# Conv plus ELU feed-forward on one core: the taps' load moves to GpSimd's queue, and the warming matmuls read another tile

## The chip, the cores and the metric

The kernel runs on one core of a Trainium2 chip. A core has TensorE (PE; matmuls and their weight loads), VectorE (DVE), ScalarE (ACT), GpSimd (POOL) and SyncE (SP, which only issues transfers). Each engine works through its own queue of instructions in order, and the queues meet at semaphores. Transfers are issued from the queues of SyncE, ScalarE and GpSimd and are carried by 16 DMA engines. The metric is the device time of one execution in microseconds, median of several runs; lower is better.

## The reference

`x` is (8, 4096, 192), `weight` (8, 7). First a depthwise causal convolution along the sequence: the 192 columns are 8 heads of 24, each head has 7 taps, which are the softmax of its row of `weight`. Then a feed-forward step over all 32768 tokens: 192 to 2048, ELU, 2048 to 192.

```python
w = np.exp(weight - np.max(weight, axis=-1, keepdims=True))
w = w / (np.sum(w, axis=-1, keepdims=True) + 1e-09)              # (8, 7)
x_pad = np.concatenate([np.zeros((B, 6, D)), x], axis=1)
out = np.einsum('hk,bskhg->bshg', w, windows of x_pad)           # 7 taps back
h = out.reshape(B * S, D) @ w_in
g = np.where(h > 0.0, h, np.exp(np.minimum(h, 0.0)) - 1.0)
return (g @ w_out).astype(np.float32)
```

## The kernel before

It is written instruction by instruction for each engine, with semaphores by hand: one function for each of the five queues. The order of TensorE's work in the steady part is a list, `steps`, made ahead of time; nothing at run time changes it.

The tokens are cut into 32 tiles of 1024. Each tile passes 16 blocks of 128 columns of the hidden layer; a step n is one block of one tile, in two halves of 512 tokens (u = 0, 1). For each half, TensorE makes `H` by three matmuls (`w_in` against `att`, line 754), ScalarE takes its exponential into `E` (line 543), GpSimd cuts it at 1 (line 471), VectorE takes the larger of `E - 1` and `H` into `gT` (line 610), and TensorE multiplies `gT` by `w_out` (line 788) into `ops`, which ScalarE copies out. `H` has six banks of PSUM, so TensorE may be ahead of VectorE by six halves and no more.

The convolved tokens `att` of tiles 1 to 31 come from matmuls of `x` (`xg`) with a band matrix `Tm` of the taps (line 732), copied by ScalarE (line 521) and turned by a transposing transfer. Those of tile 1 stand in TensorE's queue at steps 7 to 10, those of tile 2 from step 13.

The first tile goes another way, so that it starts early. This is the part that matters here; the line numbers are of the kernel before:

- The first 1024 rows of x come in two loads of 512 rows into `xf` (`load_first`, line 340): ScalarE's queue issues the first half as its first instruction, SyncE's queue the second half, behind the load of the taps (`wh`, line 802; 8 rows of 28 bytes).
- VectorE begins with memsets: `zw` (zeros, 128 x 512, line 553), `sel`, `ident`, and three more. GpSimd makes an identity matrix of `ident` and a selection matrix of `sel` (lines 431 and 440), then waits for the taps (line 449), and then issues its loads in this order: `w_in` in three column groups of two loads each (line 425), both pieces of x of tile 1 (`xg`, line 398), `w_out` (line 455), both pieces of x of tile 2. Only then comes its loop of cutting at 1.
- The softmax of the taps: VectorE takes the row maximum (line 562, waits for the taps) and subtracts it (564), ScalarE takes the exponential (488), VectorE makes the reciprocal (568) and the tap tile `zt` (570). In ScalarE's queue the exponential stands ahead of the cast of its half of x (490); in VectorE's queue these four stand ahead of the cast of its half (578).
- SyncE writes `zw` and then `zt` into a DRAM tensor (lines 805, 810) and reads it back as the band matrix `Tm` (815).
- TensorE: 18 warming matmuls (line 639) whose results nobody reads; one small matmul that spreads the taps over the partitions (646, waits for `zt` and for GpSimd's two selects); 12 small matmuls for the halos (652, wait for ScalarE's cast); 24 transposes of x (665, wait for VectorE's cast); two more warming matmuls; 48 conv matmuls in three groups of 16 (686), which wait for VectorE's diagonal matrices `Dg` (580) and for copies of the transposed x (499 on ScalarE, 587 on VectorE); then the list `steps`. In its first seven blocks the list also has 12 warming matmuls (line 704), which read `zw`.

The warming matmuls of line 639 read a constant tile of ones, which the program makes before the block begins:

```python
WARM = (18, 1, 2)
one = nc.const_aps.tensor(1.0, [P, HP * QUAD], BF16)     # 128 x 256
```

`W(sem, value)` makes the engine wait until a semaphore has reached a value; a wait that is already known to be met is left out.

Of the kernel before, what the change touches and what calls it, by code (L numbers as in the profile page):

```python
# [8 lines left out]
BF16 = mybir.dt.bfloat16  # L9
# [3 lines left out]
P = 128  # L13
HP = 64
# [22 lines left out]
RUN = 2  # L37
WCOLS = ((0, 256), (256, 1024), (1024, 2048))
Q_PART = (0,) * 2 + (1,) * 6 + (2,) * 8
WARM = (18, 1, 2)  # L40

CONV_AT = ((0, 1, 1, 0), (4, 1, 1, 1), (9, 2, 0, 0), (12, 2, 0, 1))
EARLY_CONV = ((7, 1, 0, 0), (8, 1, 0, 1), (9, 1, 1, 0), (10, 1, 1, 1), (13, 2, 0, 0), (14, 2, 0, 1))
# [4 lines left out]
QUAD = 4  # L48
# [6 lines left out]
def bass_lightweight_conv__then__act_elu_kernel(  # L55
# [167 lines left out]
    with ExitStack() as stack:  # L223
# [32 lines left out]
        zw = sbuf("zw", [P, GS], BF16)  # L256
# [136 lines left out]
        @block.gpsimd  # L393
        def _gpsimd(g: bass.BassGpSimd):
            W = Waits(g)

            def load_x(s, part):
                g.dma_start(  # L398
                    xg[:, s % NXB, WPG * part : WPG * (part + 1), :],
                    bass.AP(  # L400
                        tensor=x_flat.tensor,
                        offset=(s * SUP + GS * part - PAD) * D,
                        ap=[[D, P], [TOK * D, WPG], [1, D]],
                    ),
                ).then_inc(s_x[s % NXB][part], 16)

            def pad_x(s):
                x_ready(W, s, 0)
                g.memset(xg[0:PAD, s % NXB, 0, :], 0.0).then_inc(s_z)

            def copy_x(s):
                W(s_cv, 4 * (s - NXB - 1) + 1)
                if s == NXB + 1:
                    g.dma_start(  # L414
                        xb[s * SUP - 8 : s * SUP, :], x_flat[s * SUP - 8 : s * SUP, :]
                    ).then_inc(s_xb[s % 2], 16)
                g.dma_start(  # L417
                    xb[s * SUP : (s + 1) * SUP, :].rearrange("(p t) d -> p (t d)", p=P),
                    x_flat[s * SUP : (s + 1) * SUP, :].rearrange("(p t) d -> p (t d)", p=P),
                ).then_inc(s_xb[s % 2], 16)  # L420

            def load_w_in(k, halves):
                c0, c1 = WCOLS[k]
                for r in halves:
                    g.dma_start(  # L425
                        w_in[HP * r : HP * (r + 1), :, c0:c1],
                        moe_w_in.rearrange("(p j) f -> p j f", j=3)[:, :, c0:c1],
                    ).then_inc(s_w[k], 16)

            W(s_one, 1)  # L430
            g.affine_select(
                out=ident[:],
                in_=ident[:],
                pattern=[[-1, P]],
                compare_op=ALU.is_equal,
                fill=0.0,
                base=0,
                channel_multiplier=1,
            ).then_inc(s_id)
            g.affine_select(  # L440
                out=sel[:].rearrange("p (r h c) -> p r h c", r=2, h=HEADS),
                in_=sel[:].rearrange("p (r h c) -> p r h c", r=2, h=HEADS),
                pattern=[[0, 2], [-1, HEADS], [0, 8]],
                compare_op=ALU.is_equal,
                fill=0.0,
                base=0,
                channel_multiplier=1,
            ).then_inc(s_id)
            W(s_wd, 16)
            load_w_in(0, (0, 1))  # L450
            load_w_in(1, (0, 1))
            load_w_in(2, (0, 1))
            load_x(1, 0)
            load_x(1, 1)
            g.dma_start(
                w_out.rearrange("p (q r) d -> p q (r d)", r=RUN),
                moe_w_out.rearrange("(q p r) d -> p q (r d)", p=FC, r=RUN),
            ).then_inc(s_w[3], 16)
            load_x(2, 0)
            load_x(2, 1)  # L460
            for n in range(NP):
                s, i = divmod(n, NQ)
                if i == X_PAD and s + 2 < NS and (s + 2) % SPB == 0:
                    pad_x(s + 2)
                if i == X_COPY and s and s + 3 < NS:
                    copy_x(s + 3)
                if n == X_LATE[0]:
                    copy_x(3)
                for u in range(2):
                    W(s_exp, 2 * n + u + 1)  # L470
                    g.tensor_scalar(  # L471
                        out=E[:, n % NE, u, :],
                        in0=E[:, n % NE, u, :],
                        scalar1=1.0,
                        scalar2=0.0,
                        op0=ALU.min,
                        op1=ALU.max,
                    ).then_inc(s_clp)
# [141 lines left out]
        def _tensor(pe):  # L620
# [11 lines left out]
                else:  # L632
                    W(s_ce, 2 * was[1] + was[2] + 1)

            one = nc.const_aps.tensor(1.0, [P, HP * QUAD], BF16)

            def warm(count):
                for _ in range(count):
                    pe.matmul(  # L639
                        ops[:, 0, 0 : HP * QUAD], one[:, 0:P], one, start=True, stop=True  # L640
                    )

            warm(WARM[0])
            W(s_id, 2)
# [17 lines left out]
            for j in range(3):  # L662
# [8 lines left out]
                            tile_position=(0, HP * r),  # L671
                        )
                ins.then_inc(s_tp)
            warm(WARM[2])
            W(s_D, 1)
            W(s_z0, 2)
            for j in range(3):
# [18 lines left out]
                            tile_position=(HP * r, 0),  # L696
                        )
                ins.then_inc(s_hc)
            W(s_zw, 1)
            seen = {}  # L700
            for x_, op in enumerate(steps):
                if op[0] == "w":
# [96 lines left out]
        @block.sync  # L799
        def _sync(sy):  # L800
            W = Waits(sy)
            sy.dma_start(wh[:], weight[:, :]).then_inc(s_wd, 16)
            load_first(sy, 1)
            W(s_zw, 1)
            sy.dma_start(
                bass.AP(tensor=taps.tensor, offset=0, ap=[[(HEADS + 2) * CW, BANDS], [(HEADS + 1) * CW, 2], [1, CW]]),
                zw[0:BANDS, 0 : 2 * CW].rearrange("p (a e) -> p a e", a=2),
            ).then_inc(s_band, 16)
            W(s_wp, 1)
            sy.dma_start(  # L810
                bass.AP(tensor=taps.tensor, offset=CW, ap=[[CW, HEADS], [(HEADS + 2) * CW, BANDS], [1, CW]]),
                zt[:, :].unsqueeze(1).to_broadcast([HEADS, BANDS, CW]),
            ).then_inc(s_band, 16)
            W(s_band, 32)
            sy.dma_start(
                Tm[:, :, :].rearrange("p h e -> p (h e)"),
                bass.AP(tensor=taps.tensor, offset=CW + TAP + KSIZE - 1, ap=[[(HEADS + 2) * CW - P // BANDS, BANDS], [-1, P // BANDS], [1, HEADS * CW]]),
            ).then_inc(s_band, 16)

            def load_cast(s):  # L820
                W(s_cv, 4 * (s - NXB))
                W(s_xb[s % 2], 16 * ((s - 1) // 2 + (s % 2)))
                if s > NXB + 1:
                    W(s_xb[(s - 1) % 2], 16 * ((s - 2) // 2 + ((s - 1) % 2)))
                for part in range(2):
                    row = s * SUP + GS * part - PAD
                    for w0, w1, rows in ((0, WPG - 1, P), (WPG - 1, WPG, GS - TOK * (WPG - 1) + PAD)):
                        v0 = WPG * part
                        sy.dma_start(
                            xg[0:rows, s % NXB, v0 + w0 : v0 + w1, :],  # L830
                            bass.AP(
                                tensor=xb.tensor,
                                offset=(row + TOK * w0) * D,
                                ap=[[D, rows], [TOK * D, w1 - w0], [1, D]],
                            ),
                        ).then_inc(s_xq[s % NXB][part], 16)

            for x_, op in enumerate(steps):
                if op[0] == "h" and op[2:] == (0, 0):
                    s, i = divmod(op[1], NQ)  # L840
                    if i == X_LOAD and s and s + 3 < NS:
                        load_cast(s + 3)
                    if op[1] == X_LATE[1]:
                        load_cast(3)
                elif op[0] == "c" and op[3:] == (1, HB - 1):
                    m, b = op[1:3]
                    s = m // 2 + 1
                    if m % 2 and b:
                        conv_read(W, m)
                        for u in range(2):  # L850
                            W(s_h[u], NQ * (s - 1))
                        turn_att(sy, s)
                elif x_ in stops:
                    acc = acc_of(op)
                    t, half, kb, g = acc
                    if (t, half) == (last, 1):
                        if (kb, g) != (1, 1):
                            taken(W, acc)
                            out_group(sy, t, half, g, kb)
                    else:  # L860
                        taken(W, acc)
                        out_group(sy, t, half, g)
            for b in range(2):
                sy.wait_ge(s_out[b], 32 * NS + 32 * b)
# [28 lines left out]
```

## Time and profile before

| what | value |
|---|---|
| median of 3 runs | 724.81 us (724.77 to 725.16) |
| profiled execution, its own time | 724.81 us |
| its span (first to last instruction) | 722.7 us |
| TensorE matmul busy | 716.8 us, 99% of the span |
| VectorE busy | 651.2 us, 90% |
| ScalarE busy | 655.9 us, 91% |
| GpSimd busy | 631.3 us, 87% |
| first H matmul (line 754) begins | 11.29 us |
| first E (ScalarE), first gT (VectorE) | 12.48 us, 13.82 us |
| x of the first tile used: ScalarE's half, SyncE's half | 3.88 us, 5.15 us |

Times inside the profile are counted from the first instruction of the execution. A row of the timeline gives start, length, engine, line, operation, what it writes and reads, how many instructions are merged, and in brackets how long the engine was idle before and what ended that. [...] A busy TensorE is not a TensorE at its peak. "issue" as a reason for idle time means that no engine is seen to end it; a landing transfer may be what ended it. The time from issue to landing of a transfer is in the part on DMA, as a median over the transfers in a row.

### The profile page before, as it was taken

To read this page: it belongs to the slowest core of one execution; us is meant where nothing else is said; L and a number is where in the kernel's file an instruction comes from. 1 tells how busy PE (TensorE), PEld (TensorE's weight loads), DVE (VectorE), ACT (ScalarE), POOL (GpSimd) and SP (SyncE) were. 2 spreads that over 40 slices of the span, in tenths; PEclk is the share of its full clock that TensorE was granted. 3 is DMA by queue.
4 is the path that set the end of the run, shared out by engine and by line. 5 is a ranking of instruction groups with operands and counts; after the bars stand their busy time and mean duration, and the time that the engine had idled before them with its cause. 6 is when DMAs were issued, how large, how long until landed. Compare 5 with 4: busy or idle time off the path is not lost.

```text
span 722.7 us, 28745 instructions
## 1 busy us (share of the span) xinstructions
PE 716.8 (99%) x11877; PEld 622.0 (86%) x11877; DVE 651.2 (90%) x1043; ACT 655.9 (91%) x1286; POOL 631.3 (87%) x1078
## 2 busy tenths in 40 slices
PE   9999999999999999999999999999999999999998
PEld 5598888888888888888888888888888888888897
DVE  4889999999999999999999999999999999999995
ACT  5999999999999999999999999999999999999994
POOL 7889888889888889888889888898888898888893
PEclk9999999999999999999999999999999999999999
DMA  9855533555544634344545345444346454542212
GB/s 175 128 119 84 117 71 95 117 93 93 99 87 95 116 80 106 90 97 95 113 74 110 77 95 116 100 87 111 75 95 117 87 100 97 91 94 71 57 36 68
DMA packets 130051, 69.16 MB, mean 96 GB/s; under 512 B 94128, under 2 KB 128688, under 8 KB 129456
## 3 DMA queue, kind: packets, MB, share of 16 engines
q1 hardware_dynamic: 123760, 52.08, 31.3%
q0 software_dynamic: 5872, 14.75, 15.1%
q8 instruction: 93, 1.52, 0.8%
q10 hardware_dynamic: 288, 0.49, 0.2%
q14 instruction: 38, 0.31, 0.1%
HBM read 43.51 MB, written 36.61 MB: 111 GB/s over the span
## 4 chain that ended last, share of the span: by engine, by line
PE 96%; DVE 1%; ACT 1%; POOL 1%; DMA 1%; issue 0%; SPq 0%; ACTq 0%
PE ops L788 51%; PE H L754 40%; PE H L732 3%; DVE gT L610 1%; PE H L788 1%; ACT E L543 1%; DMA xf<-in_x_dram 1%; POOL E L471 0%; PE H L686 0%; PE ops L686 0%; PE H L665 0%; ACT csb L521 0%; DVE xh L578 0%; PE ops L639 0%; POOL x_cast L414 0%
## 5 line engine op out<-in xcount | busy, mean ns | idle before, releaser
L610 DVE SCALAR_TENSOR_TENSOR gT<-E,H 128x512 f16<-128x512 f32 x1024 | 645.4, 683 | 56.3 <-POOL E L471 49.2
L471 POOL TENSOR_SCALAR E<-E 128x512 f32<-128x512 f32 x1024 | 606.1, 615 | 80.0 <-ACT E L543 76.0
L543 ACT ACTIVATE E<-H 128x512 f32<-128x512 f32 x1024 | 565.2, 612 | 49.0 <-PE H L754 44.2
L754 PE MATMUL H<-att,w_in 64*128 64x512 bf16 x3072 | 602.9, 377 | 1.2 <-DVE gT L610 1.0
L788 PE MATMUL ops<-w_out,gT 64*128 64x192 f16 x8064 | 587.1, 243 | 0.0
L788 PEld LDWEIGHTS ops<-w_out,gT 64*128 64x128 f16 x8064 | 516.5, 94 | 54.5 <-PE ops L788 29.4
L754 PEld LDWEIGHTS H<-att,w_in 64*128 64x128 bf16 x3072 | 257.5, 94 | 20.8 <-DVE gT L610 6.8
L732 PE MATMUL H<-xg,Tm 64*128 64x240 bf16 x480 | 87.6, 263 | 0.3 <-DVE gT L610 0.3
L521 ACT ACTIVATE csb<-H 128x480 bf16<-128x480 f32 x120 | 70.7, 589 | 0.0
L513 ACT ACTIVATE osb<-ops 128x384 f32<-128x384 f32 x125 | 61.0, 488 | 7.3 <-PE ops L788 5.7
L732 PEld LDWEIGHTS H<-xg,Tm 64*128 64x128 bf16 x480 | 38.3, 93 | 16.1 <-issue 0.6
L417 POOL DMA_DIRECT2D x_cast<-in_x_dram x29 | 15.7, 540 | 0.0
L788 PE MATMUL H<-w_out,gT 64*128 64x192 f16 x128 | 6.4, 243 | 0.0
L788 PEld LDWEIGHTS H<-w_out,gT 64*128 64x128 f16 x128 | 5.7, 94 | 0.0
L639 PE MATMUL ops<-const-bfloat16-1.0 128*128 128x256 bf16 x20 | 4.6, 414 | 0.8 <-PEq L878 0.8
L602 DVE COPY osb<-ops 128x384 f32<-128x384 f32 x1 | 0.6, 558 | 4.3 <-PE ops L788 4.3
L639 PEld LDWEIGHTS ops<-const-bfloat16-1.0 128*128 128x128 bf16 x20 | 2.6, 139 | 2.0 <-issue 1.0
L704 PE MATMUL ops<-zw 64*128 64x512 bf16 x12 | 4.2, 376 | 0.0
L425 POOL DMA_DIRECT2D w_in<-in_moe_w_in_dram x6 | 4.0, 679 | 0.2 <-issue 0.2
L398 POOL DMA_DIRECT2D xg<-in_x_dram x4 | 3.5, 880 | 0.0
L589 DVE CAST att<-H 128x512 bf16<-128x512 f32 x1 | 0.7, 692 | 3.0 <-PE H L686 3.0
L732 PE MATMUL ops<-xg,Tm 64*128 64x240 bf16 x16 | 3.0, 264 | 0.3 <-ACT csb L521 0.3
(49 smaller groups left out, 31.1 us busy)
## 6 DMA issues: line engine op xcount, KB each, us to landing
out_dram<-osb SPq DMA_DIRECT2D x126, 192.0 KB, 3.0
x_cast<-in_x_dram POOLq DMA_DIRECT2D x29, 384.0 KB, 5.3
xg<-x_cast SPq DMA_DIRECT2D x58, 192.0 KB
xg<-x_cast SPq DMA_DIRECT2D x58, 26.2 KB
xg<-in_x_dram POOLq DMA_DIRECT2D x4, 240.0 KB, 13.9
w_in<-in_moe_w_in_dram POOLq DMA_DIRECT2D x2, 384.0 KB, 11.0
w_out<-in_moe_w_out_dram POOLq DMA_DIRECT2D x1, 768.0 KB, 15.2
w_in<-in_moe_w_in_dram POOLq DMA_DIRECT2D x2, 288.0 KB, 6.6
```

Source lines behind the costliest of these rows:

```text
L417: g.dma_start(xb[s * SUP : (s + 1) * SUP, :].rearrange("(p t) d -> p (t d)", p=P), x_flat[s * SUP : (s + 1) * SUP, :].rearrange("(p t) d - ...
L425: g.dma_start(w_in[HP * r : HP * (r + 1), :, c0:c1], moe_w_in.rearrange("(p j) f -> p j f", j=3)[:, :, c0:c1],).then_inc(s_w[k], 16)
L471: g.tensor_scalar(out=E[:, n % NE, u, :], in0=E[:, n % NE, u, :], scalar1=1.0, scalar2=0.0, op0=ALU.min, op1=ALU.max,).then_inc(s_clp)
L513: a.activation(*out_pieces(acc), ACT.Copy).then_inc(s_oev)
L521: return a.activation(csb[:, s % 2, :].rearrange("p (j v h i) -> p h j v i", j=3, v=2 * WPG, h=HEADS)[:, h0 : h0 + HB], bank_of(("c", m, b ...
L543: a.activation(E[:, n % NE, u, :], bank_of(op[:3]), ACT.Exp).then_inc(s_exp)
L610: v.scalar_tensor_tensor(out=gT[:, s % NG3, q, u, :], in0=E[:, n % NE, u, :], scalar=1.0, in1=bank_of(op[:3]), op0=ALU.subtract, op1=ALU.m ...
L639: pe.matmul(ops[:, 0, 0 : HP * QUAD], one[:, 0:P], one, start=True, stop=True)
L704: pe.matmul(ops[:, 1 - rt, :], zw[HP * rt : HP * (rt + 1), 0:P], zw[HP * rt : HP * (rt + 1), :], start=True, stop=True, tile_position=(HP ...
L732: ins = pe.matmul(bank_of(op[:3])[:, n1 * hh : n1 * (hh + 1)], Tm[HP * rt : HP * (rt + 1), h, :], xg[HP * rt : HP * (rt + 1), s % NXB, :, ...
L754: ins = pe.matmul(bank_of(op[:3]), w_in[HP * r : HP * (r + 1), j, RUN * FC * (q // RUN) + q % RUN : RUN * FC * (q // RUN + 1) : RUN,], att ...
L788: ins = pe.matmul(to[:, d0 : d0 + D], gT[HP * rt : HP * (rt + 1), t % NG3, q, g, t0 : t0 + P], w_out[HP * rt : HP * (rt + 1), q, :], start ...
```

## The change

Two things change at the start, and nothing after it.

The load of the taps goes from SyncE's queue to GpSimd's, ahead of everything else there; SyncE's first instruction is then its half of the first x load. The line in GpSimd's queue that waits for the taps ahead of the `w_in` loads stays.

The warming matmuls read `zw` in place of the constant tile, as wide as the 12 later ones (512 columns and not 256), and wait for its memset; there are 9 of them in place of 18, and the two between the transposes and the conv matmuls are gone. The later wait of TensorE for `zw`, which is now already met, goes too.

```diff
-WARM = (18, 1, 2)
+WARM = (9, 1)
...
         def _gpsimd(g: bass.BassGpSimd):
             W = Waits(g)
+            g.dma_start(wh[:], weight[:, :]).then_inc(s_wd, 16)
...
-            one = nc.const_aps.tensor(1.0, [P, HP * QUAD], BF16)
-
             def warm(count):
+                W(s_zw, 1)
                 for _ in range(count):
-                    pe.matmul(
-                        ops[:, 0, 0 : HP * QUAD], one[:, 0:P], one, start=True, stop=True
-                    )
+                    pe.matmul(ops[:, 0, :], zw[:, 0:P], zw[:], start=True, stop=True)
...
-            warm(WARM[2])
             W(s_D, 1)
             W(s_z0, 2)
...
-            W(s_zw, 1)
             seen = {}
...
         def _sync(sy):
             W = Waits(sy)
-            sy.dma_start(wh[:], weight[:, :]).then_inc(s_wd, 16)
             load_first(sy, 1)
```

## The prediction

> **What bounds the kernel now.** I read the shares of the chain that ended last, then that chain in order of time over the first 40 us, the timeline of the first 25 us, the DMA windows, the landings of the GpSimd queue, and the matmul groups by form.
>
> The shares (engines):
> ```profile
> PE 96%; DVE 1%; ACT 1%; POOL 1%; DMA 1%; issue 0%; SPq 0%; ACTq 0%
> ```
> TensorE sets the end. The change touches nothing after the start, so the question is by how much the moment shifts from which TensorE runs without waits. The chain in order of time (start, length, what):
> ```profile
> 0.80 0.40 SPq L802
> 1.26 3.87 DMA xf<-in_x_dram
> 5.15 0.57 DVE xh L578
> 5.77 1.49 PE H L665 x24
> 7.26 0.54 PE ops L639 x2
> 7.80 1.82 PE ops L686 x16
> 9.62 1.85 PE H L686 x32
> 11.50 0.44 DVE att L594
> ...
> 26.47 0.50 ACT E L543
> 27.04 2.35 POOL E L471 x4
> ...
> 31.12 0.70 DVE gT L610
> 31.87 0.47 PE H L754 x3
> ```
> Both edits lie on it: the taps' issue holds back SyncE's x load by 0.46 us, and two warming matmuls stand between transposes and conv. From 12.5 to 31.9 us the chain runs over ScalarE, GpSimd and VectorE; then over TensorE to the end. What is late at 31.87 is late at the end.
>
> The x loads, as DMA traffic by half microseconds (last number GB/s):
> ```profile
> 2.00:2.50 0.50, 0.50 (x5) 0.30 (x4) 0.47 (x3) 0.50 (x1) 0.28 (x2) 1.00 0.88 264
> 2.50:3.00 0.50, 0.50 (x4) 0.37 (x3) 0.05 (x1) 0.46 (x5) 0.50 (x1) 1.00 1.05 363
> 3.00:3.50 0.50, 0.50 (x4) 0.36 (x3) 0.29 (x2) 0.14 (x2) 0.50 (x2) 1.00 0.89 338
> 3.50:4.00 0.50, 0.50 (x5) 0.30 (x3) 0.09 (x1) 0.12 (x1) 0.50 (x2) 1.00 1.00 399
> ```
> With 80 GB/s in 1.5 to 2.0 that is 722 KB by 4.0; the two loads are 786 KB. They already run as one stream, ending near 4.2: ScalarE's half is used at 3.88, SyncE's at 5.15.
>
> The first depthwise-conv step of the next tile, and the landing of its x (two pieces, issued 6.46 and 7.37):
> ```profile
> 19.64 0.12 PEld L732 LDWEIGHTS ops<-xg,Tm 64*128 64x128 bf16 x2 [0.20 <-issue]
> ```
> ```profile
> DMA to landing us min/median/max: 11.8/12.0/12.2
> ```
> 7.37 + 12.2 = 19.57, and TensorE's idle of 0.20 ends at 19.64 with no engine to blame. So this landing, the end of GpSimd's queue of loads, already gates TensorE.
>
> The conv matmuls by form (busy us, mean ns):
> ```profile
> L686 PE MATMUL H<-xT,Dg 64*128 64x256 bf16 x32 | 2.0, 276 | 0.0
> L686 PE MATMUL ops<-xT,Dg 64*128 64x256 bf16 x16 | 1.9, 413 | 0.0
> ```
> One form, two speeds: 8 pairs in 1.82 us (0.23 a pair), then 16 pairs in 1.85 (0.116). TensorE reaches full speed at about 9.4 us, 3.6 us after the transposes begin. (The granted clock reads 1.00 in the rows above already; I go by durations.)
>
> **Taps by GpSimd.** The issue moves from SyncE's 0.80 to the head of GpSimd's queue, also near 0.80, where GpSimd idled 1.03 us until VectorE's ident at 1.54. The nearest row:
> ```profile
> x_cast<-in_x_dram POOLq DMA_DIRECT2D x1, 3.0 KB, 2.6
> ```
> It issued in 0.59 us. Bounds for the taps: 1.35 us from issue to use (their own on SyncE's queue, used at 2.15), and 3.2 us (the first 96 KB of w_in on GpSimd's queue). I take 2.6, the only small transfer there: landed at 3.4, 1.25 later. GpSimd's two selects slip from 1.54 to at most 1.7; mask waits in VectorE's queue before the taps anyway, and TensorE asks for them only near 5.
>
> [...]
>
> *Behind the taps on VectorE and ScalarE.* From use (2.15) to the exponential's end on ScalarE (3.15) 1.0, to zt (3.58) 1.43. So ScalarE is free for its cast at about 4.4, VectorE for its at 4.85, zt is there for TensorE at 4.85. The cover is the x stream and the warming; if x came at 3.88 as now, ScalarE's cast would be 0.5 late.
>
> *Behind the taps on GpSimd.* The same wait holds the six w_in loads, x of tile 1, w_out and x of tile 2: first issue 2.43 becomes about 3.45. Data of the first w_in came about 1.7 us after its issue, just as the x stream ended; now it comes near 5.1, so the engines stand for up to 0.9 us of a stretch in which they were full. They stay full (share 0.9 to 1.55) up to 23, so this is not won back: x of tile 1 lands 0.8 later (bounds 0 and 1.05), at 20.4. Others have room: the second w_in group is first read at about 13.2 and landed at 12.15, x of tile 2 lands at 26.0 against a use at 27.6. The band matrix on SyncE goes 1.25 later with zt; the trace's landings end at 16.74 now, 18.0 then, against 19.64.
>
> *What a late conv costs.* Its matmuls stand in TensorE's queue ahead of the H matmuls that feed ScalarE, which ran without a gap from 19.39 to 21.67 and would have taken the next one at 20.53, some 0.2 after it was ready. So 0.8 less 0.2 reaches ScalarE: +0.6 (bounds 0 and +0.85). From there on the chain has no room: ScalarE to 26.97, GpSimd 27.04 to 31.1, VectorE, TensorE.
>
> **SyncE begins with x.** The issue comes 0.46 earlier, but the stream is full from 2.0, so its end stays near 4.2; only the shares change. Bounds for ScalarE's half: 3.88, as now, and 5.13, if SyncE's goes first (issues then at 0.80 and 0.81). I take about 4.7 for both. Then ScalarE's cast ends at 5.55, the 12 halo matmuls (0.75 until the next can start) at 6.35, and the transposes start at 6.4 against 5.77 (bounds 6.0 and 6.75).
>
> **Warming.** 18 x 256 columns took 0.84 to 4.77, and 9 x 512 are as many columns: 3.93 us. They wait for zw (memset ends at 1.19), so they run 1.23 to 5.16; all of TensorE's queue is behind that, but x is later still. The two matmuls after the transposes go: conv starts when the transposes end, 1.44 after they start: 7.85 against 7.80. If full speed comes at 9.4 as now, conv ends within 0.1 of now (bounds -0.3 and +0.3).
>
> **Sum.** The front moves by about 0; the conv step waits for a landing, so the larger of 0 and +0.6 counts, not both. The profiled execution took 724.81 (span 722.7, 2.1 around it), which is the median as well: 724.8 + 0.6 = 725.4. A measurement of this kernel can tell about 0.2% (1.45 us) from no change, so this is "no change". Own range of this case: 725.0 to 726.0.
>
> **The rivals.**
> *Full speed one step late (28%).* Place: the conv. Full speed came only after 3.6 us of dense matmuls from 5.77; 4.0 us of warming before, followed by the sparse halos, did not bring it. Now a hole of about 1 us (5.16 to 6.4, halos in it) precedes the transposes. If what decides is a fixed stretch that ended at 9.4 and began near 5.8, the hole breaks it when the transposes start after some 6.5. Then all 24 pairs run slow: 16 x (0.228 - 0.116) = 1.8, with the front's +0.2 some +2.0, and the landing at 20.4 is hidden: 726.8, slower. Against it: the transposes may start at 6.0, and the failed stretch held about as large a sparse part. [...]
>
> *The taps come fast (20%).* GpSimd's DMA lands in 1.35 to 1.8 us; loads slip by at most 0.4, of which 0.2 is room, and the removed 0.54 us of warming shows: 724.8 - 0.2 = 724.6. For it: only eight rows of 28 bytes. Against: 2.6 at 29.3 us.
>
> *The taps come late (6%).* Their few packets wait behind x on full engines, past 4.3; conv waits 1.8 longer: 724.8 + 1.6 = 726.4.
>
> *Full speed early (3%).* The warming, ending 0.4 later, fills a stretch that failed before: the first 8 conv pairs (0.9) and half the transposes (0.7) gain, -1.5: 723.3.
>
> **How the numbers follow.** Forecast 43%: 725.4. Faster by over 0.2%: the last rival and a little of the fast taps, 0.04. Slower by over 0.2% (above 726.26): late speed 0.28, late taps 0.06, the forecast's upper end 0.02: 0.36. The rest 0.60. The range takes in the fast taps and the late speed's centre: 724.5 to 727.0; left out are the early speed and the tails.
>
> **What would show it.** Right: first use of the taps at 3.2 to 3.6; first w_in issue at about 3.45; the idle before the first conv step of tile 1 at 0.8 to 1.0 instead of 0.20, ending near 20.4; transposes at 6.0 to 6.75; the 32-conv group still near 276 ns. Wrong: that group near 413 (late speed), taps used before 2.7 (fast taps), or the conv step's idle unchanged with all queues later.

## The result, and the profile after

The changed kernel takes 730.08 us (729.92 to 730.36) against 724.98 for the kernel before beside it: 1.007 times as long, 95% interval 1.0053 to 1.0088. It is 5.1 us slower, where the forecast was +0.6. The profiled execution took 730.23 (span 728.1), so the difference to explain in the two profiles is 730.23 - 724.81 = 5.4 us.

The shares of the chain that ended last, by engine:

```profile
PE 95%; DMA 2%; POOL 1%; ACT 1%; issue 0%; DVE 0%; ACTq 0%; POOLq 0%
```

The DMA share is 2% where it was 1%: two transfers of 4.15 and 13.54 us stand in the chain, where one of 3.87 stood. The same chain in order of time (start, length, what):

```profile
1.34 4.15 DMA wh<-in_weight_dram
5.49 0.30 issue
5.79 3.97 POOL w_in L426 x6
9.76 0.89 POOL xg L399
10.65 13.54 DMA xg<-in_x_dram
24.19 0.14 issue
24.33 0.26 PE ops L728
...
31.62 2.35 POOL E L472 x4
...
36.44 0.47 PE H L750 x3
```

The chain no longer goes through the first x load, the transposes and the conv. It goes from the taps (`wh`, 4.15 us from issue to landing) to GpSimd's queue, through six w_in loads and one x load that stand behind the taps there, to the landing of x of tile 1 at 24.19, and from there into the conv step. 36.44 stands where 31.87 stood: 4.57 us later. From the 17th on, all of the 1024 gT steps (each is VectorE's work on one half of a block) are 4.54 to 4.58 later than before: from there on nothing is won back and nothing is added.

The timeline of the changed kernel at the places that count:

```profile
1.34 0.68 POOL L396 DMA_DIRECT2D wh<-in_weight_dram  x1 [0.83 <-POOLq L873]
5.51 0.15 DVE L563 TENSOR_REDUCE whm<-wh 8x1 f32<-8x7 f32 x1 [2.77 <-DMA wh<-in_weight_dram]
6.16 0.82 ACT L491 ACTIVATE xh<-xf 128x768 bf16<-128x768 f32 x1
17.14 0.39 PE L750 MATMUL H<-att,w_in 64*128 64x512 bf16 x1 [2.22 <-DMA w_in<-in_moe_w_in_dram]
24.33 0.26 PE L728 MATMUL ops<-xg,Tm 64*128 64x240 bf16 x1 [0.83 <-DMA xg<-in_x_dram]
```

The taps are used at 5.51 and not at 2.15. GpSimd could issue only at 1.34, half a microsecond after the other queues' 0.80. ScalarE's cast of x begins at 6.16 and not at 3.88, though by the trace's landings both halves of x were there at 4.97 and 5.14: the exponential of the taps stood ahead of it. The second group of w_in, which had a microsecond of room, holds TensorE for 2.22 us. After that hole TensorE ran one stretch at half speed, by the trace's clock records from 18.20 to 21.61 (columns: stretch, its length, busy time and instructions of TensorE, weight loads, VectorE, ScalarE, GpSimd, granted clock, DMA share, GB/s):

```profile
17.90:21.30 3.40, 3.40 (x22) 1.20 (x18) 1.92 (x4) 2.43 (x5) 2.38 (x4) 0.54 1.41 193
```

All this is covered by the later wait for x: gT is 1.37 us late at its first step, 3.1 at the fifth, 3.8 at the eleventh and 4.57 at the last.

The rest is 5.4 - 4.57 = 0.85 us. Of this 0.74 comes at the very end: from the start of the last gT to the end of the span it is 9.79 us before and 10.53 now. The other 0.1 lies outside the span (2.1 us before, 2.2 now). SyncE's first two of the last five output issues, before and after:

```profile
718.42 0.89 SPq L363 DMA_DIRECT2D out_dram<-osb  x2
```

```profile
723.00 1.74 SPq L363 DMA_DIRECT2D out_dram<-osb  x2
```

The same two instructions take 1.74 us and not 0.89, and what is behind them in the queue ends the run.

### The profile page after: what moved, and what is told of

It reads as the page before. It is cut to its first block, busy times and chain, and to the rows that moved or that the text cites. A ratio compares the mean times of both kernels' runs of the same rounds, so it can differ in the third digit from the quotient of the medians.

```text
span 728.1 us, 28723 instructions
## 1 busy us (share of the span) xinstructions
PE 716.0 (98%) x11866; PEld 621.2 (85%) x11866; DVE 651.6 (89%) x1043; ACT 655.9 (90%) x1286; POOL 631.8 (87%) x1079
## 3 DMA queue, kind: packets, MB, share of 16 engines
q8 instruction: 93, 1.52, 0.9%
## 4 chain that ended last, share of the span: by engine, by line
PE 95%; DMA 2%; POOL 1%; ACT 1%; issue 0%; DVE 0%; ACTq 0%; POOLq 0%
PE ops L784 51%; PE H L750 40%; PE H L728 3%; DMA xg<-in_x_dram 2%; PE H L784 1%; DMA wh<-in_weight_dram 1%; POOL w_in L426 1%; ACT E L544 1%; POOL E L472 0%; POOL xg L399 0%; ACT csb L522 0%; DVE gT L611 0%; POOL x_cast L418 0%; POOL x_cast L415 0%; ACT osb L514 0%
## 5 line engine op out<-in xcount | busy, mean ns | idle before, releaser
L639 PE MATMUL ops<-zw 128*128 128x512 bf16 x9 | 3.7, 594 | 1.3 <-DVE zw L554 1.3
```

The lines of the kernel that those rows point to most:

```text
L639: pe.matmul(ops[:, 0, :], zw[:, 0:P], zw[:], start=True, stop=True)
```

## The experiments

The changed kernel and the kernel before differ in two parts, so the first question is which part costs.

**Taps alone.** The kernel before, with the taps' line moved to GpSimd's queue:

```diff
+            g.dma_start(wh[:], weight[:, :]).then_inc(s_wd, 16)   # first of GpSimd
-            sy.dma_start(wh[:], weight[:, :]).then_inc(s_wd, 16)
```

> Only the taps move to GpSimd's queue; the warming is as before. If the late taps are the whole cause (theory 1), the taps are again first used at about 5.5 us, the first conv step of tile 1 waits for x until about 24 us, and the time is 729.3 to 730.4. If the changed warming has a part (theory 2: fewer, later warming matmuls leave TensorE slow at the wrong moments), the time is at least 1 us below the changed kernel's 730.1.

Measured: 729.04 against 725.17 before, 1.0047 (1.0032 to 1.0062): 3.9 us slower. Taps used at 5.52, conv step at 23.92 behind 1.44 us of waiting for x. The time is 0.3 under the range expected and 1.04 under the changed kernel, so theory 2's mark is just met as well: the rest of the change costs about 1 us. The two profiled executions differ by 1.17: 0.42 of it is the conv step (gT +4.15 and not +4.57), and about 0.75 is the end, where SyncE's last issues here took 0.89 and 1.51, as before.

**Warming alone.** The changed kernel with the taps back on SyncE's queue.

> Only the warming changes; the taps stay on SyncE's queue. Theory 1: 724.5 to 725.4, as the kernel before. Theory 2: at least 1 us above 725.0.

Measured: 725.51, 1.0007 (0.9994 to 1.0019): between the two theories' marks and not clear of no change. The profile shows two things that nearly cancel. TensorE reached full speed early in this execution (by the clock records at 5.84, and at 9.64 in the kernel before), and gT began 1.50 us earlier; but x of tile 1 landed only 0.16 earlier (19.37 and not 19.53), the conv step waited for it, and 0.27 was left:

```profile
19.50 0.26 PE L727 MATMUL ops<-xg,Tm 64*128 64x240 bf16 x1 [1.27 <-DMA xg<-in_x_dram]
```

And the slow output issue at the end was there again (2.26 us for the last three, 1.51 before).

**GpSimd does not wait for the taps.** The changed kernel without the wait ahead of the w_in loads, which need nothing of the taps:

```diff
-            W(s_wd, 16)
             load_w_in(0, (0, 1))
```

> The changed kernel without GpSimd's wait for the taps ahead of its w_in loads, which need nothing of the taps. If the lateness reaches the end through GpSimd's queue of loads (theory 1a), w_in is issued at about 2.8 us, the conv step of tile 1 is gated at 20 to 21 us, and what is left is the front's 1.4 us or less: 725.5 to 726.6. If it reaches the end through the softmax of the taps and the x casts behind it (theory 1b), the time stays within 1 us of 730.1.

Measured: 728.21, 1.0035 (1.0024 to 1.0046). That is 1.9 us better than the changed kernel but not what theory 1a expected, nor 1b. The loads were early: x of tile 1 landed at 18.8, before the 19.5 of the kernel before. The conv step came at 22.16 all the same, because the band matrix was late:

```profile
22.16 0.27 PE L727 MATMUL ops<-xg,Tm 64*128 64x240 bf16 x1 [0.67 <-DMA Tm<-conv_taps]
```

SyncE's queue of the same run tells why. It writes the 32 KB of `zt` to DRAM and issues the next load when they have landed:

```profile
6.85 0.31 SPq L804 DMA_DIRECT2D conv_taps<-zt  x1
15.76 0.66 SPq L809 DMA_DIRECT2D Tm<-conv_taps  x1
```

8.9 us for 32 KB. In the changed kernel the same two issues are at 6.71 and 8.86 (2.15 us), in the kernel before at 3.61 and 6.07 (2.46). In those two, two w_in loads had been issued on GpSimd's queue when the small transfer came; here it was all six and one x load. By the DMA records its first packet started 4.45 us after the issue, and its 128 packets were spread over the next 3.9 us, among those of GpSimd's loads. The run of the next experiment, with five w_in loads issued ahead of it, took 8.0 us for the same transfer; the eleven kernels with two or three took 2.1 to 3.6. No run varied that count alone. So there is a third path from late taps to the conv step, through SyncE, and it opens as soon as GpSimd's loads no longer wait.

**Why the taps are late: x waits for them.** The changed kernel, both x loads behind the taps:

```diff
+            W(s_wd, 16)
             load_first(a, 0)
...
+            W(s_wd, 16)
             load_first(sy, 1)
```

> The changed kernel, but both x loads of the first tile wait for the taps, so that the taps' transfer has the DMA engines to itself. If the taps were late because their few packets stood behind the x stream (theory A), they are first used at 2.8 to 3.5 us. If the first transfer on GpSimd's queue is slow by itself (theory B), they are used at 5.0 us or later again. The time itself is no measure here: x comes later.

```profile
3.27 0.15 DVE L564 TENSOR_REDUCE whm<-wh 8x1 f32<-8x7 f32 x1 [0.54 <-DMA wh<-in_weight_dram]
```

Used at 3.27: theory A. With the engines to itself the transfer takes 1.9 us from its issue at 1.33. Behind the x stream it took 4.15. (The one run took 729.22; x comes late.)

**Half of the stream.** Only SyncE's half of x waits:

> The changed kernel, but only SyncE's x half waits for the taps: half of the x stream is ahead of the taps' packets. If the taps wait until what is queued on the DMA engines has drained (theory A), their first packet moves with the amount: between 2.7 us (no stream, measured) and 4.3 us (both halves), near 3.3, and they are first used at 3.6 to 4.1. If any x stream at all holds them back by a fixed time (rival), they are used at 5.2 to 5.6 as with both halves.

```profile
4.18 0.15 DVE L563 TENSOR_REDUCE whm<-wh 8x1 f32<-8x7 f32 x1 [1.45 <-DMA wh<-in_weight_dram]
```

Used at 4.18, 0.1 above the range of theory A and far from the rival's 5.2. By the trace's DMA records the taps' first packet starts at 2.70 with no x ahead of it, 3.08 with 384 KB, 4.27 to 4.54 with 768 KB (four kernels; 4.27 in the changed one). The few packets, 224 bytes in all, start late in the stream issued 0.5 us before them: in the changed kernel 215 of the 256 packets of x had ended by 4.27. (One run, 728.94 us.)

**The end: the count of matmuls.** The changed kernel has 11 matmuls fewer than the kernel before. This one adds 11 of 8 columns behind the warming, while TensorE waits for the taps anyway:

```diff
             warm(WARM[0])
+            for _ in range(11):
+                pe.matmul(ops[:, 0, 0:8], zw[:, 0:P], zw[:, 0:8], start=True, stop=True)
```

> The changed kernel with 11 small matmuls (8 columns, results unread) behind the 9 warming ones, while TensorE waits for the taps anyway: TensorE's program then has as many matmuls as before. If the last 0.8 us of the loss come from where TensorE's 16 KB code fetch falls against SyncE's last output issues (theory C), all last five issues of SyncE take under 0.55 us and the time is 728.9 to 729.6. If the slow issue at the end has another cause (rival: it came with the later queue positions or by chance), the time stays 729.8 to 730.4.

```profile
722.99 0.89 SPq L363 DMA_DIRECT2D out_dram<-osb  x2
```

Measured: 729.46 (728.56 to 730.05), 1.0053 (1.0035 to 1.007), 0.6 below the changed kernel, with intervals that overlap. gT is 4.57 late as in the changed kernel, and the issue at the end is short again. Of 13 profiles, all five with 11 matmuls fewer have one issue of 1.28 to 1.63 us among SyncE's last five; none of the eight with the old count has one over 0.5. The trace's DMA records show fetches of 16 KB on an instruction queue, every 5 to 9 us near the end and 0.9 to 1.7 us long. In the kernel before the last one starts 5.24 us before the end of the span and is over 4.28 before it, just after SyncE's first output issue (4.32 before the end); in the changed kernel it starts 4.67 before the end, and the slow issue starts 4.64 before it. That queue carried 1.52 MB in 93 fetches. If all of it is code of TensorE's 23,754 matmuls and weight loads, each has 64 bytes, and 11 matmuls with their loads are 1.4 of 16 KB, some 0.6 us of a spacing of 7 (an estimate from these counts); the last fetch did move by 0.57.

That the slow issue goes with the count of matmuls is shown by this run and by two later ones that add the same eleven. That the fetch is what makes it slow is argued: in all five the slow issue starts 0.03 to 0.09 us after a fetch, but elsewhere in these runs issues that start as close behind a fetch took 0.37 us as well as 1.3 to 1.8.

**Taps on ScalarE's queue.** The kernel before, but the taps go first on ScalarE's queue and SyncE begins with its x half:

> The kernel before with the taps as the first transfer of ScalarE's queue in place of SyncE's; SyncE begins with its x half, as in the change, and the warming is as before. If only the taps' place behind the x stream on GpSimd's queue costs (theory A), taps are used at about 2.1 to 2.6 us and the time is 724.5 to 725.6. If SyncE's early x load is itself harmful (rival: it takes the engines from everything else), the time is 726.5 or more.

```profile
4.09 0.56 DVE L579 CAST xh<-xf 128x768 bf16<-128x768 f32 x1
```

```profile
5.32 0.84 ACT L491 ACTIVATE xh<-xf 128x768 bf16<-128x768 f32 x1 [1.59 <-DMA xf<-in_x_dram]
```

Measured: 725.85, 1.0009 (0.9998 to 1.0020): a little above the range of theory A, and not clear of no change. The taps landed at 2.14, as before. The halves of x changed places: SyncE's, first now, is used at 4.09 and ScalarE's at 5.32 (before: 5.15 and 3.88). ScalarE's cast takes 0.84 against VectorE's 0.56, and the halos come behind it; gT was 0.8 late in this profile. How much of that is the order of the halves stays open: full speed was also recorded later here, from 10.52 and not 9.64. In this run an early x load of SyncE gained nothing.

**Better versions.** Four tries start from the kernel before or from the warming alone. First, x of tile 1 loaded ahead of the last w_in:

```diff
-            load_w_in(2, (0, 1))
             load_x(1, 0)
             load_x(1, 1)
+            load_w_in(2, (0, 1))
```

> The kernel before with GpSimd's loads of x of tile 1 ahead of the last two w_in loads. If the landing of x gates TensorE at 19.6 us in the kernel before, x lands near 15, the conv step no longer waits for it, and the time falls by 0.2 to 1.2 us, to 723.9 to 724.9. If that wait was covered, the time stays within 0.2 us of before. If the last w_in (then landing near 19.6) comes too late for step 8, the time rises.

```profile
19.29 0.36 PE L732 MATMUL ops<-xg,Tm 64*128 64x240 bf16 x2
```

Measured: 724.74, 0.9991 (0.9978 to 1.0003): 0.18 below, not clear of no change. x landed at 16.35 and the conv step came at 19.29 without a wait, but gT was 0.14 earlier at its first step already and 0.17 earlier at its last. So in the kernel before the wait for the landing at 19.53 was covered, the second case of the expectation (the median alone would fit the first as well): it held TensorE for 0.20 and cost the end next to nothing. Then the two warming matmuls behind the transposes cut to 8 columns as well:

> The kernel before with x of tile 1 loaded ahead of the last two w_in loads, and the two warming matmuls after the transposes cut from 256 columns to 8 (the count of matmuls stays). Those two stood 0.45 us on the front's chain, and x no longer gates at 19.6: 0.3 to 0.6 us below the same order with full-size ones, 724.0 to 724.5 as a median. If they were needed for TensorE's full speed, it is slower than that kernel.

Measured: 724.52, 0.9992 (0.9983 to 1.0000), gT 0.58 earlier in the profile, 0.57 of it from the first step on. It is the lowest median, at the edge of what can be told; against the kernel before beside it, it is no better than the run above (0.9991), so the gain expected over that order does not show. Then the warming alone with the 11 small matmuls, and that with the new order:

> Taps on SyncE's queue, the changed warming, and 11 small matmuls (8 columns) so that the count of matmuls is that of the kernel before. If the changed warming's only loss was the slow output issue at the end (theory C), this is 0.6 to 0.9 us below the warming alone (725.5) and at or a little below the kernel before: 724.4 to 725.0. If the warming itself costs, it stays at 725.3 or more.

> The last kernel with x of tile 1 loaded ahead of the last two w_in loads as well. Where the front is early it is no longer held at 19.6 us: 723.3 to 724.5, below the kernel before in most runs. If the late w_in takes over as the gate (landing near 20 us, needed at step 8), no gain over the kernel without this order.

```profile
19.94 0.26 PE L729 MATMUL ops<-xg,Tm 64*128 64x240 bf16 x1 [1.47 <-DMA xg<-in_x_dram]
```

Measured: 725.45, 1.0006 (0.9997 to 1.0015), and 724.91, 0.9996 (0.9987 to 1.0005). The first lies where its expectation puts a warming that itself costs, the second above the range expected. The first had no long issue at the end of its profile, but the time stayed that of the warming alone: gT began 1.26 early, the conv step waited 1.47 us for x (the row above), and gT ended 0.19 late. So the 0.7 to 0.8 us at the end are seen in the profiles and in the pair above, while in this pair of medians they do not show; their mean size stays open. In the profile of the second, gT began 1.05 early and ended 1.27 late: five of the taps' eight packets started at 2.55 to 2.76 and not near 1.75, though SyncE issued them first; GpSimd's loads came 1 us late behind them, and the w_in loads held TensorE for 2.35 us.

## Why the prediction was wrong

- *What bounds the kernel, and that a shift at 31.87 goes to the end:* right. +4.57 there, +4.57 at the last gT.
- *Taps by GpSimd:* the step that failed, the lag of the taps in the sum. I put 2.6 us from issue to landing from a small transfer at 29.3 us, bounds 1.35 to 3.2, and an issue at 0.80. Measured: 4.15 from an issue at 1.34. Alone on the engines it is 1.9 (its first packet 1.37 after the issue) and within the bounds; what I took for a property of the queue was one of the traffic. I had shown the x stream as continuous from 2.0 to 4.2 us and did not ask what a transfer issued into it would meet. The rival "the taps come late" names the mechanism but puts it at 6% and +1.6. The +0.6 of the sum grew out of this lag and came to +4.57.
- *GpSimd's issue:* it stood 0.54 later than the other queues' first transfers. No row of before showed a first transfer there.
- *Behind the taps on GpSimd:* the mechanism was right, the size was not: first w_in issue +3.36 and not +1.0; x of tile 1 landed at 24.19 and not at 20.4. The landing slipped by 4.6, more than the x load's issue (3.3): x took 13.5 us from issue to landing and not 12.2. Why it took longer these runs do not show. The upper bound of 1.05 rested on the lag of the taps alone and left no place for that.
- *"Others have room":* the second w_in group had 1.05 us, and a lag of 3.4 spent it: 2.22 us of waiting. It did not add to the end, since the conv step waited later still.
- *The larger of front and conv counts, not both:* right. The conv step is 4.66 late and gT 4.57; the front's 1.37 is hidden in it. The room at the conv step was 0.1 in this profile and not 0.2. That the landing "already gates TensorE" held for TensorE's 0.20 of idle, not for the end, as x loaded earlier showed.
- *SyncE begins with x:* that the earlier issue does not end the stream earlier held (landings at 4.97 and 5.14, before 5.13 for the last). With the taps late it did not matter.
- *Warming:* its run of 1.23 to 5.16 was forecast, it was 1.25 to 4.98. That it costs little held (1.0007 alone, not clear of no change). That it changes the count of matmuls, and that the last 16 KB fetch then starts 4.67 and not 5.24 us before the end, I had not thought of; the slow issue that goes with the count is the 0.74 at the end.
- *Full speed one step late:* not what happened in the changed kernel. Full speed is recorded from 4.55 us in its profile and half speed again from 7.96, after TensorE waited for the taps; the 32 conv matmuls took 306 ns in the mean, between the two speeds. That was free, behind the taps. With the taps alone full speed came at 13.31 and gT began 2.75 late, hidden behind the taps as well.
- *The taps come fast (20%):* no run shows the 0.4 us by which this rival has the loads slip. With the engines to itself the taps' transfer was used 1.94 us after its issue (1.33 to 3.27), and the first w_in issue came 1.11 later than in the kernel before (3.54 and not 2.43); behind the x stream it came 3.36 later.
- *Full speed early (3%):* where the taps were not moved, the changed warming did show the gain of about 1.5 us that this rival gives the front (gT 1.50 and 1.26 early at its first step). The wait for x of tile 1 took nearly all of it. One profile for each kernel does not tell whether the warming or the moment of the clock's step brought it. Nor do the first runs of the kernel before give its spread: later ones lie between 724.08 and 727.83.

## What to carry to other kernels

Price a transfer that is moved by what is already queued on the DMA engines when it is issued, not by its size or by the same transfer at a quiet moment: here 224 bytes took 4.15 us from issue to landing behind 768 KB of x, and 1.9 with the engines to themselves. A few bytes on which three engines wait belong ahead of the big loads, on the queue that can issue first (here 0.80 us on SyncE's and 1.34 on GpSimd's). Then follow each queue that waits for it separately, since taking one wait away (GpSimd's) made another path (SyncE's band matrix) the gate: the conv step came at 22.16 us though x had landed at 18.8. For gains below 1 us at the start, look at the next landing that holds the critical engine: an earlier front was worth only the room up to that (gT 1.50 us early with the warming alone, 0.27 left behind the wait for x).

## What the runs showed of the hardware

- The taps waited for what other queues had issued before: their 224 bytes started 2.70, 3.08 and 4.27 us into the run behind none, 384 and 768 KB of x. Another small transfer, the 32 KB of `zt`, took 2.15 us with two loads issued on GpSimd's queue and 8.9 with seven, though no run varied that count alone. An x load is 128 packets of 3 KB in the trace's records, the taps are 8 of 28 bytes. These runs do not show where they waited.
- TensorE's granted speed changed at moments that lie whole multiples of 3.41 us apart in the clock records of the changed kernel (4.55, 7.96, 11.38, 18.20 and 21.61 us), and these moments fall differently in the four profiles: full speed was first recorded at 9.64 (before), 4.55 (changed), 13.31 (taps alone) and 5.84 (warming alone). In the changed kernel half speed was recorded from 7.96 to 11.38, after 1.85 us without matmuls (4.98 to 6.83), and from 18.20 to 21.61, after 2.22 us (14.91 to 17.14); after 0.83 us (23.50 to 24.33) none was recorded before 728.17. That these holes are what lost the speed was not shown by a run that varies them alone.
- The mean length of a matmul in a row is not its cost in a stream: the 32 conv matmuls of the kernel before have 276 ns each and are 2.0 us of busy time together, where 32 such lengths add up to 8.8.
- With 11 matmuls fewer at the start one of SyncE's last five output issues took 1.28 to 1.63 us and not 0.37 to 0.49, in five profiles of five, and it started 0.03 to 0.09 us after a 16 KB fetch on an instruction queue.
